# PSUM banks held by name in the second half of an attention and MLP kernel, and a last product in two banks

## The chip, the cores and the metric

The kernel runs on one core of one Trainium2 chip. The metric is the device time of one execution in microseconds (us), the median of several runs. The engines are called as in the profile: PE is TensorE (matrix products), PEld its weight loads, DVE is VectorE, ACT is ScalarE, POOL is GpSimd, SP is SyncE, which here only issues transfers.

## What is computed

Attention over a sliding window of 128 positions with a linear distance penalty, for 8 batches of 8 heads, 576 positions and a head width of 64; then, on the joined heads (512 wide), a normalised two-layer MLP with a residual:

```python
scores = scale * np.matmul(q, k.transpose(0, 1, 3, 2))
...
scores = np.where(mask, scores + bias[None], -1000000000.0)
...
attn = attn / (np.sum(attn, axis=-1, keepdims=True) + 1e-09)
return np.matmul(attn, v).astype(np.float32)
...
xn = (x - mu) / np.sqrt(var + 1e-06) * g_ln
ch = np.maximum(xn @ w_ch1, 0.0) @ w_ch2
return (x + ch).astype(np.float32)
```

## The kernel before

The 8 x 576 rows are cut into 36 blocks of 128 rows. The batches go in pairs; the ninth block of a pair holds the 64 tail rows of both batches. The blocks are gathered in twelve groups: six of two blocks, then six of four (`GROUPS`, L26). Groups are counted from 0 here, so groups 6 to 11 have four blocks.

The program is a woven one. TensorE's order, and that of ACT and DVE, is the order in which the Python code issues instructions (the manual schedule at L847 and L848). For each group, `mlp1` makes the 16 hidden tiles (L656) and a second function makes the output; both are generators that yield after each piece of matmuls. `weave_at` (L829) runs such a generator and, at listed pieces, issues the attention steps of later blocks in between: transposes of q and k, scores, the exponential on ACT, the masks on DVE, the products with the values (`values`, L415, ending in a reciprocal and a scaling on DVE), statistics, and the normalised row `xc`, which a transposing transfer turns for a later group's `mlp1`. Because all engines run in order, an instruction that waits holds up everything behind it on its engine.

In groups 6 to 11 the second layer is `fast_mlp2` (L735). It computes a 2 by 2 block product with seven products instead of eight (Winograd's scheme): sums of hidden quarters are made on DVE (`combine_hidden`, L720, eight half sums a group), sums of weight quarters once beforehand. The seven products are, in order: x, y, z, x, z, x, w. A product is 16 matmuls at L757: for each of two row blocks, 8 matmuls of 128x256 that accumulate into half a PSUM bank (a bank is 128 x 512 fp32). x collects three products, z two, y and w one each. Between them DVE adds the bank into the output tile (`add`, L767, L770), each time 128x512: x and y into one quarter, z into another, and so on. So a later product on the same bank must wait until the add before it has read the bank. The output rows go out through `send` and `store` (L777, L819), every store issued by SP, two for a block.

PSUM has eight banks. Four (`ps_sc`) are for scores and transposes of q and k. The other four are the pool `ps_mm` (L96, four buffers, tag "mm"): each hidden tile of `mlp1` (`ps_m1`, L663), each of the two value tiles of a block (`ps_pv`, L428) and each of x, y, z and w (`ps_f`, L754) takes a buffer of this pool when it is first written, and the pool decides which. In groups 6 to 10 before the change x, y, z and w came to lie in the four different banks, with value tiles in between in the banks that were free.

The order on DVE during the first products, in groups 6 to 9: scaling of the values, two hidden sums, the two masks of a block, its statistics, the add of x, a hidden sum, the row xc, the add of y, a hidden sum, the add of z.

Of the kernel before, what the change touches and what calls it, by code (L numbers as in the profile page):

```python
# [2 lines left out]

# [1 line left out]

# [6 lines left out]
FP32 = mybir.dt.float32  # L12
# [5 lines left out]
P = 128  # L18
# [6 lines left out]
HALF = P // 2  # L25
GROUPS = [2] * 6 + [4] * 6  # L26
# [32 lines left out]
def kernel(  # L59
# [10 lines left out]
    nc = tc.nc  # L70
    B, H, S, D = q.shape
    DM = H * D
# [66 lines left out]
    QF, QD = NFB // 2, DM // 2  # L139
# [181 lines left out]
    def turn_first():  # L321
# [11 lines left out]
            copy(out=k[:, b].rearrange("p h (c r) -> p r h c", r=2), in_=ps[b])  # L333
        nc.vector.tensor_copy(out=g_row, in_=ps_row)

    weights_of, unmasked, scored = {}, {}, []

    def in_halves(t):
# [80 lines left out]
    def values(p, blk, hg):  # L419

        if hg == 0:
            n = p * NSLOT + blk
            if n % 2 == 0:
                x_pairs[n // 2] = x_pool.tile([P, 2, DM], FP16, tag="x", name="x")
            xs[p, blk] = x_pairs[n // 2][:, n % 2, :]
            if n < BY_DMA:
                sums[p, blk] = small.tile([P, 2], FP32, tag="sum", name="sum")
        ps = ps_mm.tile([P, 4, D + 1], FP32, tag="mm", name="ps_pv")  # L428
        terms = weights_of[p, blk]
        for i in range(4):  # L430
            h = 4 * hg + i
            for n, (pr, t, o) in enumerate(terms):
                nc.tensor.matmul(  # L433
                    ps[:, i, :],
                    pr[:, h, t, :],
                    vext[(p * NSLOT + o) % NV][:, h, :],
                    start=(n == 0),
                    stop=(n == len(terms) - 1),
                )
        rec = small.tile([P, 4], FP32, tag="rec", name="rec")  # L440
        nc.vector.reciprocal(out=rec, in_=ps[:, :, D])  # L441
        nc.vector.scalar_tensor_tensor(  # L442
            out=xs[p, blk][:, hg * 4 * D : (hg + 1) * 4 * D].rearrange(
                "p (h d) -> p h d", h=4
            ),
            in0=ps[:, :, 0:D],
            scalar=1.0,
            in1=rec.unsqueeze(2).broadcast_to([P, 4, D]),
            op0=ALU.mult,
            op1=ALU.mult,  # L450
            **(
                dict(accum_out=sums[p, blk][:, hg : hg + 1])
                if (p, blk) in sums
                else {}
            ),
        )
# [199 lines left out]
    def mlp1(g, on_dve=()):  # L656
        xT = turned_x[g]
        w = w1 if g < FIRST_GROUPS else w1g
        cols = len(members[g]) * P
        ht = hidden[g] = hidden_pool.tile([P, NFB, 4 * P], FP16, tag="ht", name="ht")  # L660
        turn_about = chain(*zip(range(QF), range(QF, NFB)))
        for u, fb in enumerate(turn_about if g >= FAST else range(NFB)):
            ps = ps_mm.tile([P, 4 * P], FP32, tag="mm", name="ps_m1")  # L663
            for kb in range(NKB):
                nc.tensor.matmul(  # L665
                    ps[:, 0:cols],
                    w[:, kb, fb * P : (fb + 1) * P],
                    xT[:, kb, 0:cols],
                    start=(kb == 0),
                    stop=(kb == NKB - 1),  # L670
                )
            if u in on_dve:
                nc.vector.tensor_scalar(
                    out=ht[:, fb, 0:cols],
                    in0=ps[:, 0:cols],
                    scalar1=0.0,
                    scalar2=None,
                    op0=ALU.max,
                )
            else:  # L680
                nc.scalar.activation(  # L681
                    out=ht[:, fb, 0:cols], in_=ps[:, 0:cols], func=AF.Relu
                )
            yield cols
            if g >= FAST and u == 10:
                for i in range(4):
                    combine_hidden(g, 0, i)
# [47 lines left out]
    def fast_mlp2(g):  # L735

        pairs = len(members[g]) // 2
        n0 = sum(GROUPS[:g])
        outs = [out_pool.tile([P, 2, DM], FP32, tag="o", name="o") for _ in range(2)]

        def rows(i):
            if pairs == 1:
                return x_pairs[n0 // 2][:, i : i + 1, :], outs[0][:, i : i + 1, :]
            return x_pairs[n0 // 2 + i], outs[i]

        banks = {}  # L750

        def product(name, lhs, rhs, first):
            if first:
                banks[name] = ps_mm.tile([P, 2, QD], FP32, tag="mm", name="ps_f")  # L754
            for pair in range(pairs):
                for fb in range(QF):
                    nc.tensor.matmul(  # L757
                        banks[name][:, pair, :],
                        lhs[:, fb, pair * P : (pair + 1) * P],
                        rhs[:, fb, :],  # L760
                        start=(first and pair == 0 and fb == 0),
                        stop=(fb == QF - 1),
                        skip_group_check=True,
                    )
                yield DM

        def add(name, i, j, to_x):  # L767
            x, o = rows(i)
            cols = slice(j * QD, (j + 1) * QD)
            nc.vector.tensor_tensor(  # L770
                out=o[:, :, cols],
                in0=banks[name][:, 0:pairs, :],
                in1=(x if to_x else o)[:, :, cols],
                op=ALU.add,
            )

        def send(i):  # L777
            _, o = rows(i)
            for at in range(pairs):
                store(*members[g][i * pairs + at], o[:, at, :])  # L780

        a = [[hidden_quarter(g, i, j) for j in range(2)] for i in range(2)]
        s = [hidden_sum(g, i) for i in range(4)]
        combine_hidden(g, 1, 0)
        combine_hidden(g, 1, 1)
        yield from product("x", a[0][0], quarter(0, 0), True)
        add("x", 0, 0, True)
        combine_hidden(g, 1, 2)
        yield from product("y", a[0][1], quarter(1, 0), True)
        add("y", 0, 0, False)  # L790
        combine_hidden(g, 1, 3)
        yield from product("z", s[0], t1, True)
        add("z", 1, 1, True)
        yield from product("x", s[1], t2, False)
        add("x", 0, 1, True)
        yield from product("z", s[3], quarter(1, 1), False)
        add("z", 0, 1, False)
        send(0)
        yield from product("x", s[2], t3, False)
        add("x", 1, 0, True)  # L800
        add("x", 1, 1, False)
        yield from product("w", a[1][1], t4, True)
        add("w", 1, 0, False)
        send(1)

    def finish(p, blk, ps):
        n = p * NSLOT + blk
# [8 lines left out]
        )  # L816
        store(p, blk, o)

    def store(p, blk, o):  # L819
        for b, t0, w, p0 in spans(p, blk):  # L820
            dst, src = out[b, t0 : t0 + w, :], o[p0 : p0 + w, :]
            if blk == T:
                nc.sync.dma_start(out=dst, in_=src)
            else:
                dst = dst.rearrange("(c r) d -> r c d", r=2)
                for r in range(2):
                    nc.sync.dma_start(out=dst[r], in_=src[r * HALF : (r + 1) * HALF])

    def weave_at(units, *places, also=()):  # L829
        for u, _ in enumerate(units):  # L830
            advance_to(done + places.count(u))
            if u in also:
                next(combined, None)
# [13 lines left out]
    with tc.manual_schedule(engines={engine.PE}):  # L847
        with tc.manual_schedule(engines={engine.Activation, engine.DVE}):  # L848
            advance_to(first)
            weave_at(mlp1(0, (0, 1)), 2, 7, 8, 9, 13)  # L850
            weave_at(mlp1(1), 2, 8, 12)
            weave_at(mlp2(0, ((0, 8), (8, 12), (12, NFB))), 0, 1, 3, 4, 4, 5)
            weave_at(mlp2(1), 0, 1, 2, 3, 4, 6, 6)
            weave_at(mlp1(2), 0, 3, 3, 6, 8, 11)
            weave_at(mlp2(2), 0, 2, 4, 6, 7)


            weave_at(mlp1(3, (9, 10, 11)), 8, 8, 12, 13)
            weave_at(mlp2(3), 0, 1, 1, 2, 4, 4, 5, 6)
            weave_at(mlp1(4), 0, 4, 8, 10, 10, 14)  # L860
            weave_at(mlp2(4), 0, 2, 2, 3, 5, 7, also=(1, 4, 6))
            weave_at(mlp1(5), 0, 1, 4, 8, 10, 12, also=(3, 6, 9))
            weave_at(mlp2(5), 0, 1, 2, 4, 6, 7)
            for g in range(6, len(GROUPS)):
                weave_at(
                    mlp1(g), 0, 2, 5, 7, 8, 10, 13, 15, also=(1, 4) if g == 6 else ()
                )
                weave_at(fast_mlp2(g), 1, 3, 6, 7, 7, 9, 12, 13)
# [31 lines left out]
```

## Time and profile before

| what | us |
|---|---|
| median of 3 runs | 334.84 (334.58 to 335.43) |
| the profiled execution's own time | 334.56 |
| its span, first to last instruction | 332.8 |
| `mlp1` matmuls with 512 columns (L665, 640) | 116.9 busy, 1.1 idle before |
| `fast_mlp2` matmuls (L757, 384 + 192 + 96) | 45.8 + 22.5 + 11.5 busy, 8.7 idle before |
| the adds out of PSUM in `fast_mlp2` (L770, 24 + 24) | 16.4 + 16.4 busy |
| stores (72), issue to landing | 2.4 |

Busy time is the time in which an engine had an instruction running; idle before a group of instructions is the time its engine stood still just ahead of them, with the engine that ended the wait. The mean granted clock of TensorE over the span is 0.99 of full speed. A matmul of 128x512 starts 0.216 us after the one before it, one of 128x256 0.109 us.

### The profile page before, as it was taken

Reading aid. Unit: us, or ns where it says so; the run is one execution under the profiler, and the core shown is the slowest. Engines: PE = TensorE matmul, PEld = TensorE weight load, DVE = VectorE, ACT = ScalarE, POOL = GpSimd, SP = SyncE. Lnnn points to the kernel's source line nnn. Section 1 sums busy time; section 2 is a strip of 40 time slices with the busy share of each in tenths; the row PEclk is TensorE's granted clock in tenths of the full one; section 3 lists DMA queues with packets and bytes.
Section 4 is the critical chain, followed back from the end, with each engine's and each line's share of the span. In section 5 each row is a group of like instructions: output and inputs, shape, how many; then the busy total and the mean of one; then the engine's idle time right before and its main releaser. Section 6 shows DMA issues by size and latency. Waiting matters only on the chain.

```text
span 332.8 us, 10421 instructions
## 1 busy us (share of the span) xinstructions
PE 309.3 (93%) x4478; PEld 208.2 (63%) x4478; DVE 234.4 (70%) x555; ACT 184.6 (55%) x320; POOL 114.8 (35%) x188
## 2 busy tenths in 40 slices
PE   8889999998999999999799979999899979999992
PEld 3478556757567575558655866567656854685582
DVE  2879777786777887669775986589758975761462
ACT  6688666676656583684278533763287218405600
POOL 8933677666425652813252541300000000000000
PEclk9999999999999999999999997999999999999998
DMA  9999999999599696996396966351430033015005
GB/s 112 167 207 191 189 152 195 173 140 146 47 145 96 76 157 58 160 66 65 42 164 86 97 65 98 85 43 18 81 81 18 18 80 82 18 23 121 0 2 126
DMA packets 101728, 32.34 MB, mean 97 GB/s; under 512 B 92849, under 2 KB 97073, under 8 KB 101682
## 3 DMA queue, kind: packets, MB, share of 16 engines
q0 software_dynamic: 79872, 18.36, 64.9%
q1 hardware_dynamic: 21810, 13.32, 19.4%
q8 instruction: 35, 0.57, 0.8%
q14 instruction: 11, 0.09, 0.1%
HBM read 36.90 MB, written 9.44 MB: 139 GB/s over the span
## 4 chain that ended last, share of the span: by engine, by line
PE 71%; DVE 10%; ACT 7%; POOL 4%; DMA 4%; issue 2%; DVEq 0%; POOLq 0%; ACTq 0%
PE ps_m L665 31%; PE ps_f L757 21%; PE ps_m L698 9%; ACT probs L389 4%; DMA w<-in_moe_w_ch_dram 4%; PE ps_sc L381 4%; PE ps_pv L433 4%; PE ps_sc L277 2%; DVE probs L400 2%; DVE st L530 2%; POOL vx L223 1%; DVE o L770 1%; POOL q L213 1%; DVE k L297 1%; POOL rstd L488 1%
## 5 line engine op out<-in xcount | busy, mean ns | idle before, releaser
L665 PE MATMUL ps_m<-xT,w1g 128*128 128x512 f16 (+1 forms) x640 | 116.9, 337 | 1.1 <-ACT ht L681 0.8
L681 ACT ACTIVATE ht<-ps_m 128x512 f16<-128x512 f32 (+1 forms) x187 | 89.2, 497 | 39.6 <-PE ps_m L665 36.7
L665 PEld LDWEIGHTS <-w1g 128*128 128x128 f16 x640 | 60.1, 98 | 48.8 <-issue 1.8
L389 ACT ACTIVATE probs<-ps_sc 128x1024 f16<-128x1024 f32 x56 | 54.3, 1026 | 39.7 <-PE ps_sc L381 39.7
L757 PE MATMUL ps_f<-w,ht 128*128 128x256 f16 x384 | 45.8, 279 | 8.7 <-DVE o L770 8.7
L757 PEld LDWEIGHTS <-ht 128*128 128x128 f16 x384 | 37.9, 100 | 14.9 <-issue 9.4
L485 POOL TENSOR_TENSOR rstd<-moments,powers 128x1 f32<-128x1 f32 x28 | 5.4, 192 | 118.6 <-DVE moments L531 118.6
L698 PE MATMUL ps_m<-w,ht 128*128 128x512 f16 x192 | 46.0, 380 | 0.0
L223 POOL DMA_DIRECT2D vx<-in_v_dram x40 | 34.7, 880 | 26.7 <-PE ps_pv L433 12.5
L400 DVE TENSOR_TENSOR probs<-probs,m 128x1024 f16<-128x1024 f16 x56 | 37.4, 688 | 9.1 <-ACT probs L389 8.7
L213 POOL DMA_DIRECT2D q<-in_q_dram x40 | 27.3, 688 | 20.2 <-PE ps_sc L277 12.0
L442 DVE SCALAR_TENSOR_TENSOR x<-ps_pv,rec 128x256 f16<-128x256 f32 x72 | 30.6, 425 | 2.5
L213 POOL DMA_DIRECT2D k<-in_k_dram x40 | 26.9, 686 | 5.9 <-DMA w<-in_moe_w_ch_dram 3.6
L698 PEld LDWEIGHTS <-ht 128*128 128x128 f16 x192 | 17.1, 98 | 17.4
L472 DVE TENSOR_SCALAR xc<-x,moments,rstd 128x512 f16<-128x512 f16 x28 | 11.5, 412 | 19.9 <-POOL rstd L488 19.9
L530 DVE BATCH_NORM_STATS2 st<-x 128x6 f32<-128x512 f16 x36 | 24.6, 685 | 0.0
L296 ACT COPY q<-ps_sc 128x512 f16<-128x512 f16 x15 | 8.8, 586 | 28.0 <-PE ps_sc L277 27.8
L381 PE MATMUL ps_sc<-q,k 64*64 64x128 f16 (+1 forms) x1088 | 20.4, 208 | 3.8 <-ACT probs L389 1.1
L441 DVE RECIPROCAL rec<-ps_pv 128x4 f32<-128x4 f32 x72 | 12.7, 176 | 15.9 <-PE ps_pv L433 15.5
L757 PE MATMUL ps_f<-w,hs 128*128 128x256 f16 x192 | 22.5, 273 | 0.0
L770 DVE TENSOR_TENSOR o<-ps_f,x 128x512 f32<-128x512 f32 x24 | 16.4, 684 | 7.6 <-PE ps_f L757 7.5
L433 PEld LDWEIGHTS <-probs 128*128 128x128 f16 x448 | 18.7, 97 | 4.7 <-DVE probs L400 0.3
(79 smaller groups left out, 345.5 us busy)
## 6 DMA issues: line engine op xcount, KB each, us to landing
out_dram<-o SPq DMA_DIRECT2D x72, 128.0 KB, 2.4
q<-in_q_dram POOLq DMA_DIRECT2D x32, 128.0 KB, 5.2
k<-in_k_dram POOLq DMA_DIRECT2D x32, 128.0 KB, 5.6
vx<-in_v_dram POOLq DMA_DIRECT2D x32, 128.0 KB, 6.5
w<-in_moe_w_ch_dram POOLq DMA_DIRECT2D x8, 512.0 KB, 10.7
q<-in_q_dram POOLq DMA_DIRECT2D x8, 64.0 KB, 4.7
k<-in_k_dram POOLq DMA_DIRECT2D x8, 64.0 KB, 4.5
vx<-in_v_dram POOLq DMA_DIRECT2D x8, 64.0 KB, 5.9
```

What stands on the lines that cost most here:

```text
L213: nc.gpsimd.dma_start(out=t[b * n // 2 : (b + 1) * n // 2], in_=src[2 * p + b, :, i * P : i * P + n, :].rearrange("h (c r) d -> c h r d", ...
L223: nc.gpsimd.dma_start(out=vx[p0 : p0 + n, :, 0:D], in_=v[b, :, t0 : t0 + n, :].rearrange("h p d -> p h d"),)
L381: nc.tensor.matmul(in_halves(ps[cols, j, n, t, :])[:, r, queries], kt[rows, hp, cols], in_halves(qt[rows, b, hp])[:, r, queries], start=Tr ...
L389: nc.scalar.activation(out=dst.rearrange("p (n j) q -> p j n q", j=2), in_=ps.rearrange("p j n t q -> p j n (t q)"), func=AF.Exp, scale=in ...
L400: nc.vector.tensor_tensor(out=dst, in0=dst, in1=mask, op=ALU.mult)
L433: nc.tensor.matmul(ps[:, i, :], pr[:, h, t, :], vext[(p * NSLOT + o) % NV][:, h, :], start=(n == 0), stop=(n == len(terms) - 1),)
L442: nc.vector.scalar_tensor_tensor(out=xs[p, blk][:, hg * 4 * D : (hg + 1) * 4 * D].rearrange("p (h d) -> p h d", h=4), in0=ps[:, :, 0:D], s ...
L530: nc.vector.bn_stats(out=st, in_=xs[order[n]])
L665: nc.tensor.matmul(ps[:, 0:cols], w[:, kb, fb * P : (fb + 1) * P], xT[:, kb, 0:cols], start=(kb == 0), stop=(kb == NKB - 1),)
L681: nc.scalar.activation(out=ht[:, fb, 0:cols], in_=ps[:, 0:cols], func=AF.Relu)
L698: nc.tensor.matmul(sums[at], ht[:, fb, at * P : (at + 1) * P], w2[:, fb, :], start=(fb == 0), stop=(fb == NFB - 1),)
L757: nc.tensor.matmul(banks[name][:, pair, :], lhs[:, fb, pair * P : (pair + 1) * P], rhs[:, fb, :], start=(first and pair == 0 and fb == 0), ...
```

## The change

From group 6 on, the four buffers of `ps_mm` are allocated once, as four tiles that are never given back (`ring`), and a function `psum` hands them out: the first of the list, which then goes to its end. Hidden tiles and value tiles take the next of the list. At the start of `fast_mlp2` the first two become the bank of x and the bank of y, and **z uses the bank of y**; the other two stay in the list for value tiles, and w is written into the first of those. Behind the sixth product the list is put together again: second other bank, y, x, first other bank.

In the last group w's two halves go to two different banks, its add is made in two halves of 128x256, and the last two blocks are stored by columns: the right halves after the sixth product, the left half of each block after its add. These stores are issued by SP and ACT in turn. All other stores stay with SP.

```diff
+    ring = []
+    def psum(name, banks=None):
+        if not ring:
+            return ps_mm.tile([P, DM], FP32, tag="mm", name=name)
+        t = (banks or ring)[0]
+        if banks is None:
+            ring.append(ring.pop(0))
+        return t
...
-        ps = ps_mm.tile([P, 4, D + 1], FP32, tag="mm", name="ps_pv")
+        ps = psum("ps_pv")[:, 0 : 4 * (D + 1)].rearrange("p (h d) -> p h d", h=4)
...
-            ps = ps_mm.tile([P, 4 * P], FP32, tag="mm", name="ps_m1")
+            ps = psum("ps_m1")
...
-        banks = {}
+        x_bank, y_bank, *others = ring
+        use = dict(x=[x_bank] * 2, y=[y_bank] * 2, z=[y_bank] * 2, w=others[:1] * 2)
+        if g == len(GROUPS) - 1:
+            use["w"] = others
+        ring[:] = others
+        banks = {
+            name: [b.rearrange("p (j d) -> p j d", j=2) for b in bs]
+            for name, bs in use.items()
+        }
...
-            if first:
-                banks[name] = ps_mm.tile([P, 2, QD], FP32, tag="mm", name="ps_f")
...
-                        banks[name][:, pair, :],
+                        banks[name][pair][:, pair, :],
...
-                        start=(first and pair == 0 and fb == 0),
+                        start=(
+                            first
+                            and fb == 0
+                            and (pair == 0 or use[name][0] is not use[name][1])
+                        ),
...
-        def add(name, i, j, to_x):
+        def add(name, i, j, to_x, at=slice(0, pairs)):
...
-        def send(i):
+        def send(i, ats=range(pairs), cols=slice(0, DM), queues=(nc.sync,)):
...
-        yield from product("w", a[1][1], t4, True)
-        add("w", 1, 0, False)
-        send(1)
+        if use["w"][0] is use["w"][1]:
+            ring[:] = [others[1], y_bank, x_bank, others[0]]
+            yield from product("w", a[1][1], t4, True)
+            add("w", 1, 0, False)
+            send(1)
+        else:
+            low, high = slice(0, QD), slice(QD, DM)
+            send(1, cols=high, queues=(nc.sync, nc.scalar))
+            for at, _ in enumerate(product("w", a[1][1], t4, True)):
+                add("w", 1, 0, False, slice(at, at + 1))
+                send(1, [at], low, (nc.sync, nc.scalar))
+                yield DM
...
-    def store(p, blk, o):
+    def store(p, blk, o, cols=slice(0, DM), queues=(nc.sync,)):
+        queues = cycle(queues)
...
+            ring += [ps_mm.tile([P, DM], FP32, tag="mm", name="ps_r") for _ in range(4)]
             for g in range(6, len(GROUPS)):
```

More of the change, by code (lines that the diff above doesn't have):

```diff
@@ L1 @@
 from contextlib import ExitStack
-from itertools import chain
+from itertools import chain, cycle
 import numpy as np
@@ L770, in add @@
             nc.vector.tensor_tensor(
-                out=o[:, :, cols],
-                in0=banks[name][:, 0:pairs, :],
-                in1=(x if to_x else o)[:, :, cols],
+                out=o[:, at, cols],
+                in0=banks[name][at.start][:, at, :],
+                in1=(x if to_x else o)[:, at, cols],
                 op=ALU.add,
             )
-        def send(i):
+        def send(i, ats=range(pairs), cols=slice(0, DM), queues=(nc.sync,)):
             _, o = rows(i)
-            for at in range(pairs):
-                store(*members[g][i * pairs + at], o[:, at, :])
+            for at in ats:
+                store(*members[g][i * pairs + at], o[:, at, :], cols, queues)
         a = [[hidden_quarter(g, i, j) for j in range(2)] for i in range(2)]
@@ L817, in finish @@
         store(p, blk, o)
-    def store(p, blk, o):
+    def store(p, blk, o, cols=slice(0, DM), queues=(nc.sync,)):
+        queues = cycle(queues)
         for b, t0, w, p0 in spans(p, blk):
-            dst, src = out[b, t0 : t0 + w, :], o[p0 : p0 + w, :]
+            dst, src = out[b, t0 : t0 + w, cols], o[p0 : p0 + w, cols]
             if blk == T:
-                nc.sync.dma_start(out=dst, in_=src)
+                next(queues).dma_start(out=dst, in_=src)
             else:
@@ L826, in store @@
                 for r in range(2):
-                    nc.sync.dma_start(out=dst[r], in_=src[r * HALF : (r + 1) * HALF])
+                    next(queues).dma_start(
+                        out=dst[r], in_=src[r * HALF : (r + 1) * HALF]
+                    )
     def weave_at(units, *places, also=()):
```

## The prediction

> **What bounds the kernel now.** I read the page's busy shares first, then TensorE's waits from 150 us to the end (groups of four blocks start at 135.3 us), the timeline of one group, the windows with the granted clock, and the timeline of the tail. The busy shares:
>
> ```profile
> PE 309.3 (93%) x4478; PEld 208.2 (63%) x4478; DVE 234.4 (70%) x555; ACT 184.6 (55%) x320; POOL 114.8 (35%) x188
> ```
>
> TensorE's waits after 150 us (who for whom; us in all, times, longest):
>
> ```profile
> PE ps_f L757 <- DVE o L770: 8.7, 4, 2.2
> PE ps_sc L381 <- DVE rec L441: 0.4, 1, 0.4
> ```
>
> That is 9.1 us in 183. TensorE is the bound, it runs its queue in order, and there is almost no slack into which a new wait could fall: what is added on TensorE here arrives at the end. The 8.7 us are four waits of 2.14, 2.24, 2.11 and 2.20 us, one in each of groups 6 to 9, all at the sixth product. The timeline of group 7 (start, duration, engine, line; a bracket gives the idle time before it):
>
> ```profile
> 186.06 3.67 PE L757 MATMUL ps_f<-w,ht 128*128 128x256 f16 x32
> 189.56 2.78 PE L757 MATMUL ps_f<-w,hs 128*128 128x256 f16 x24
> 189.91 0.69 DVE L770 TENSOR_TENSOR o<-ps_f,x 128x512 f32<-128x512 f32 x1
> 190.52 0.68 DVE L733 TENSOR_TENSOR w<-ht,hs 128x1024 f16<-128x1024 f16 x1
> 191.12 0.41 DVE L472 TENSOR_SCALAR xc<-x,moments,rstd 128x512 f16<-128x512 f16 x1
> 191.44 0.68 DVE L770 TENSOR_TENSOR o<-ps_f,o 128x512 f32<-128x512 f32 x1
> ...
> 198.20 0.66 DVE L770 TENSOR_TENSOR o<-ps_f,x 128x512 f32<-128x512 f32 x1
> 198.92 5.32 PE L757 MATMUL ps_f<-w,ht 128*128 128x256 f16 x32 [2.24 <-DVE o L770]
> ```
>
> The 32 matmuls at 186.06 are products x and y; z starts at 189.56 at once, since it has a bank of its own. VectorE is behind: it adds x at 189.91 and y only at 191.44 to 192.12. The sixth product (x again) waits for the add that reads x's bank, which ends at 198.86; TensorE goes on at 198.92, some 0.05 us after.
>
> **z in y's bank.** From group 6 on, z gets the bank of y. Its first matmul (start set) then cannot be issued before the add of y has read that bank; in the changed program's instruction order it carries that wait, and VectorE's order is unchanged: the add of y still stands behind the masks, the statistics, the add of x, a hidden sum and xc. So z starts 0.05 us after the add of y ends. From the timelines (z's start now; end of the add of y):
> - group 6: 155.48; 157.32 + 0.68 = 158.00: 2.57 us
> - group 7: 189.56; 192.12: 2.61
> - group 8: 225.20; 227.29 + 0.68 = 227.97: 2.82
> - group 9: 259.26; 261.24 + 0.68 = 261.92: 2.71
> - group 10: 291.98; 293.22 + 0.69 = 293.91: 1.98
> - group 11: 318.02; 318.22 + 0.69 = 318.91: 0.94
>
> Together 13.63 us. Behind z in TensorE's queue stand the fourth product, the values and scores of the next block, and the rest. Nothing takes the delay back: the sixth product's wait hangs on a chain that TensorE itself starts after the fourth product (scores, two ACT exponentials, masks, statistics, add of x). In group 6 VectorE idles 0.21 us for the values, then 0.42 and 0.22 us for ACT, so it follows TensorE there and is not working off a backlog; the chain moves with z and the 8.7 us stay.
>
> **The w bank in the next group.** w takes the first of the two other banks, and the ring afterwards is values' bank, y, x, w. Behind w come two values tiles, so the next group's first hidden tile goes to x and its second to w's bank. VectorE adds w only after the values. The second tile would start four matmuls of 0.216 us (0.864) after the first: at 170.25, 205.98, 239.93 and 273.96 for groups 7 to 10; the adds end at 170.56, 206.30, 240.24 and 274.38. With 0.05 us each: 0.36 + 0.37 + 0.36 + 0.47 = 1.56 us. Before, that bank came fourth in groups 7 to 10, 1.7 us later, which hid the add; that cover is gone. Group 11 has no values behind w, its fourth tile takes w's bank, and it costs nothing there.
>
> **The held tiles.** With one tile per bank for the rest of the program, a reciprocal also waits for the ACT that read its bank before: always long done, but one more semaphore instruction on VectorE, two per values step. The rows for such instructions run 21 to 50 ns. The two before z in each of groups 6 to 10 lie on VectorE's way to the add of y: between 0 and 10 x 0.05 = 0.5 us; I take 0.25. The ACT ones are hidden in the 0.27 us ACT idles between two hidden tiles.
>
> **The tail.** Timeline of the last group's end:
>
> ```profile
> 324.18 4.60 SPq L827 DMA_DIRECT2D out_dram<-o  x6
> ...
> 325.82 0.68 DVE L770 TENSOR_TENSOR o<-ps_f,o 128x512 f32<-128x512 f32 x1
> 326.96 0.69 DVE L770 TENSOR_TENSOR o<-ps_f,o 128x512 f32<-128x512 f32 x1 [0.46 <-PE ps_f L757]
> 328.83 1.24 SPq L823 DMA_DIRECT2D out_dram<-o  x2
> ```
>
> The last add ends at 327.65; SP then issues four stores one after the other (0.6 us and a small step each), the last at 329.48, which lands 2.4 us later. After the change the last product's halves lie in two banks, the first half is added beside the second's matmuls, and the add that remains is 128x256 (estimate 0.40 us, near the 0.42 us of the 128x256 row that reads PSUM on L442): done at 327.36. Eight stores of half the bytes go out, four on each queue. SP is busy with the stores of the first two blocks until 326.58, then issues at about 326.6, 327.25, 327.9 and 328.55: 0.93 us earlier than 329.48. No trace row has ACT issuing a transfer. If it costs what SP's do, ACT ends with SP; if it costs POOL's 0.88 us (L223), its fourth starts near 326.55 + 3 x 0.9 = 329.25 and only 0.23 is saved; if also the smaller transfer lands 0.3 us sooner than 2.4 (estimate), 1.25 is saved. SP's rows are the nearer ones, the same stores out of the same tiles, where POOL's are loads with a change of type: I take 0.95.
>
> **The clock.** Windows of 3.41 us, laid so that the stretch at half clock fills one (busy us by engine, then the granted clock):
>
> ```profile
> 162.25:165.66 3.41, 1.56 (x15) 1.40 (x15) 2.77 (x6) 0.00 (x0) 0.74 (x2) 1.00 0.46 27
> 196.38:199.79 3.41, 1.17 (x12) 0.89 (x11) 2.78 (x7) 0.36 (x1) 0.97 (x3) 1.00 0.93 68
> 199.79:203.20 3.41, 3.41 (x19) 2.43 (x17) 1.75 (x3) 0.00 (x0) 0.00 (x0) 0.50 0.49 102
> 230.51:233.92 3.41, 1.91 (x21) 1.57 (x17) 2.86 (x8) 1.84 (x2) 0.00 (x0) 1.00 0.00 0
> ```
>
> In group 7 the 2.24 us gap fell whole into one window (TensorE busy 1.17 of 3.41), and the next window ran at 0.50: 32 matmuls took 5.32 us where groups 8 and 9 show 3.65. That is 1.67 us. The other three gaps straddled a window's edge (busy 1.56 and more) and cost none. So the limit lies between 1.85 and 2.24 us idle in a window; I take 2.05. A gap of g us at a random phase has that much in one window with chance (3.41 + g - 4.10)/3.41: 0.58 for the four new gaps (mean 2.68), 0.43 for the four old ones (2.17), none for 1.98 and 0.94. That is 2.3 + 1.7 = 4.1 slow windows where before had one: 3.1 more; with the limit at 2.24, 2.4 more, at 1.86, 4.0. Before drew one where this formula gives 1.7, and its times lie within 0.9 us of each other, less than a slow window's cost; so I take the low side, 2.5 more: 2.5 x 1.67 = 4.2 us, with 0 and 7 x 1.67 = 11.7 as ends.
>
> The Trainium skill ("TensorE: Matmul & The Clock Gate", section "Why this matters for your kernels") asks only that TensorE not idle longer than about 3 us between bursts; by it none of these gaps would cost clock and the sum would be 349.0. The trace differs: 2.24 us were enough. The same page's section "A second HAM failure mode: psum-queue depth-cycling" speaks against this change: cycling through PSUM banks with small TensorE gaps made the clock swing there. The half-speed window after the gap agrees with it.
>
> **Sum**, against the profiled execution's 334.56 us (its span 332.8 and 1.8 around it; 0.28 under the median of 334.84): 334.56 + 13.63 + 1.56 + 0.25 - 0.95 = 349.05; + 4.2 for the clock = 353.3 us.
>
> **Rivals.**
> - The same waits, clock no worse: 349.0. For it: three of the four old gaps cost nothing. Against: the new gaps are 0.4 us longer, and there are four more.
> - A slow window after nearly every gap: 349.05 + 11.7 = 360.7. Against: three of four now go free.
> - The new wait replaces the old one: if the add of x in the fourth product's wake hung on VectorE's own backlog, TensorE would find it done: 349.05 - 8.7 = 340.4. For it: VectorE works without a break from 185.4 to 194.2 in group 7. Against: the idle gaps for values and ACT just before that add.
> - Not slower: the add of y is through before z wants its bank. It decides only if VectorE gets there 2.5 us sooner than now; then 13.63 and 0.25 fall away, 334.56 + 1.56 - 0.95 = 335.2, and without w's wait 333.6. Against: VectorE's order is the same and its row back to back. This is also the case in which the new bank names bind nothing.
>
> **How the numbers follow.** Forecast 353.3: 0.58, its own range 350.5 to 357.5. Clock no worse 0.20, slow windows everywhere 0.10, wait replaced 0.09, not slower 0.03. The range 347.8 to 357.5 takes in the first two and, with the tail's 0.23 to 1.25 and the semaphores' 0 to 0.5, leaves the rest out, about 0.2. About 0.3% (1 us) is what a measurement here tells from no change. Faster by more than that (333.6): 0.01; within it (335.2): 0.02; slower: 0.97.
>
> **What would show it.** Right: TensorE waits for the add on z's first matmul, six times, 13 to 14 us, the longest in groups 6 to 9; the four old waits still near 2.2 us; four of about 0.4 us at a group's second hidden tile; three or four windows at 0.50; last stores issued by SP and ACT, the last about 1 us nearer to the last matmul. Wrong: the waits at the sixth product shrink as those at z grow; or no wait at z; or the time beyond 357.5 with more slow windows than four.

## The result and the profile after

The changed kernel took 353.52 us (median of four runs: 348.92, 351.00, 356.04, 357.52). Beside it the kernel before took 334.71 (median of four). The ratio is 1.047, with an interval of 1.037 to 1.057; it leaves out the two slower of the four runs, which lie over 1.5% above the fastest, so it comes out below the ratio of the two medians. The profiled execution is the longest of the four, 357.52 us with a span of 355.7.

The page of the changed kernel, its busy shares, the row of the granted clock and two groups of matmuls (busy, mean ns of one, idle time before and who ended it):

```profile
PE 319.1 (90%) x4478; PEld 211.9 (60%) x4478; DVE 235.8 (66%) x556; ACT 184.9 (52%) x320; POOL 114.8 (32%) x188
...
PEclk9999999999999999988899899998999889999999
...
L775 PE MATMUL ps_r<-w,ht 128*128 128x256 f16 x384 | 49.0, 290 | 8.7 <-DVE o L792 8.7
...
L775 PE MATMUL ps_r<-w,hs 128*128 128x256 f16 x192 | 27.1, 307 | 12.9 <-DVE o L792 12.9
```

The matmuls are as many as before (4478). The busy time of PE is 9.8 us longer with the same work, most of it a slower clock; all dips of the clock's row lie in the groups of four. The 8.7 us of waiting ahead of the products that read `ht` (all at the sixth) are unchanged, and 12.9 us have come up ahead of the products that read `hs`, where before had none. z is the first of these.

TensorE's waits of the changed kernel from 150 us on (who for whom; us in all, times, longest):

```profile
PE ps_r L775 <- DVE o L792: 21.7, 10, 2.7
PE ps_r L677 <- DVE o L792: 0.9, 4, 0.3
PE ps_sc L393 <- DVE rec L453: 0.4, 1, 0.4
```

The ten waits at the products are the four old ones and six new ones. The four on L677 are the second hidden tile of groups 7 to 10. Group 7 in the timeline of the changed kernel (start, duration, engine, line; the bracket is the idle time before it):

```profile
192.39 3.67 PE L775 MATMUL ps_r<-w,ht 128*128 128x256 f16 x32
...
196.32 0.69 DVE L792 TENSOR_TENSOR o<-ps_r,x 128x512 f32<-128x512 f32 x1
196.93 0.68 DVE L745 TENSOR_TENSOR w<-ht,hs 128x1024 f16<-128x1024 f16 x1
197.52 0.41 DVE L484 TENSOR_SCALAR xc<-x,moments,rstd 128x512 f16<-128x512 f16 x1
197.84 0.69 DVE L792 TENSOR_TENSOR o<-ps_r,o 128x512 f32<-128x512 f32 x1
198.45 0.68 DVE L745 TENSOR_TENSOR ht<-ht 128x1024 f16<-128x1024 f16 x1
198.58 4.45 PE L775 MATMUL ps_r<-w,hs 128*128 128x256 f16 x24 [2.52 <-DVE o L792]
...
209.60 3.65 PE L775 MATMUL ps_r<-w,ht 128*128 128x256 f16 x32 [2.24 <-DVE o L792]
```

DVE does the same things in the same order as before: the add of x, a hidden sum, xc, and only then the add of y (197.84 to 198.53). z starts 0.05 us after that add, where before it followed the y product at once. The sixth product, 11 us later, still waits its 2.24 us.

Windows of 3.41 us of the changed kernel, laid against the stretches at half clock (busy us of PE, PEld, DVE, ACT and POOL, then the granted clock, DMA share and GB/s):

```profile
164.85:168.26 3.41, 1.39 (x13) 1.09 (x12) 2.73 (x6) 1.35 (x2) 0.62 (x3) 1.00 0.67 46
168.26:171.67 3.41, 3.29 (x16) 2.30 (x16) 1.08 (x3) 0.00 (x0) 0.40 (x1) 0.50 0.21 41
195.57:198.98 3.41, 0.89 (x9) 0.65 (x7) 3.38 (x7) 0.00 (x0) 0.75 (x2) 1.00 0.34 20
198.98:202.39 3.41, 3.41 (x18) 2.46 (x17) 0.69 (x2) 0.00 (x0) 0.00 (x0) 0.50 0.22 43
...
311.60:315.03 3.43, 1.55 (x15) 1.24 (x14) 3.37 (x8) 0.00 (x0) 0.74 (x2) 1.00 0.00 0
315.03:318.44 3.41, 3.41 (x34) 3.05 (x32) 0.98 (x2) 0.00 (x0) 0.00 (x0) 1.00 0.20 38
```

Up to the last matmul, six windows of this execution ran at half clock, against one in the profiled execution of before. Ahead of each of the six stood a window in which TensorE was busy for 0.89 to 1.39 us (1.20, 1.39, 0.89, 1.29, 1.18, 1.21); the windows with 1.55 us or more had none behind them.

The tail of the changed kernel (the queues' rows show when a store is issued and how long that takes):

```profile
349.55 1.56 DVE L792 TENSOR_TENSOR o<-ps_r,o 128x512 f32<-128x512 f32 x3
350.26 0.57 ACTq L859 DMA_DIRECT2D out_dram<-o  x1
...
352.22 0.56 ACTq L855 DMA_DIRECT2D out_dram<-o  x1
352.50 0.56 SPq L855 DMA_DIRECT2D out_dram<-o  x1
```

An issue by ACT takes 0.55 to 0.61 us, like one by SP. From the end of the last matmul to the end of the span it is 5.09 us (350.65 to 355.74) where before took 5.87 (326.92 to 332.79).

### The profile page after: what moved, and what is told of

Read it like the earlier page. It is cut to its first block, busy times and chain, and to the rows that moved or that the text cites. A ratio compares the mean times of both kernels' runs of the same rounds, so it can differ in the third digit from the quotient of the medians.

```text
span 355.7 us, 10469 instructions
## 1 busy us (share of the span) xinstructions
PE 319.1 (90%) x4478; PEld 211.9 (60%) x4478; DVE 235.8 (66%) x556; ACT 184.9 (52%) x320; POOL 114.8 (32%) x188
## 4 chain that ended last, share of the span: by engine, by line
PE 56%; DVE 23%; ACT 6%; DMA 5%; POOL 5%; issue 4%; DVEq 0%; POOLq 0%; ACTq 0%
PE ps_r L677 17%; PE ps_r L775 17%; PE ps_m L710 8%; PE ps_m L677 7%; ACT probs L401 4%; DVE probs L412 4%; DMA w<-in_moe_w_ch_dram 4%; DVE hs L745 3%; DVE st L542 3%; DVE o L792 3%; PE ps_sc L393 2%; DVE x L454 2%; PE ps_sc L277 2%; PE ps_r L445 2%; DMA q<-in_q_dram 1%
## 5 line engine op out<-in xcount | busy, mean ns | idle before, releaser
L677 PEld LDWEIGHTS <-w1g 128*128 128x128 f16 x640 | 60.1, 98 | 50.3 <-issue 3.8
L677 PE MATMUL ps_r<-xT,w1g 128*128 128x512 f16 x384 | 86.1, 380 | 0.9 <-DVE o L792 0.9
L693 ACT ACTIVATE ht<-ps_r 128x512 f16<-128x512 f32 x96 | 56.4, 599 | 33.6 <-PE ps_r L677 33.6
L775 PE MATMUL ps_r<-w,ht 128*128 128x256 f16 x384 | 49.0, 290 | 8.7 <-DVE o L792 8.7
L775 PEld LDWEIGHTS <-ht 128*128 128x128 f16 x384 | 39.4, 104 | 16.8 <-issue 9.4
L775 PE MATMUL ps_r<-w,hs 128*128 128x256 f16 x192 | 27.1, 307 | 12.9 <-DVE o L792 12.9
L693 ACT ACTIVATE ht<-ps_m 128x256 f16<-128x256 f32 x91 | 33.1, 388 | 9.2 <-PE ps_m L677 6.5
L677 PE MATMUL ps_m<-xT,w1g 128*128 128x256 f16 x256 | 31.4, 273 | 1.1 <-ACT ht L693 0.8
L792 DVE TENSOR_TENSOR o<-ps_r,x 128x512 f32<-128x512 f32 x24 | 16.5, 686 | 23.1 <-PE ps_r L775 23.1
L775 PEld LDWEIGHTS <-hs 128*128 128x128 f16 x192 | 20.7, 109 | 18.4 <-issue 14.0
L710 PEld LDWEIGHTS <-ht 128*128 128x128 f16 x192 | 17.1, 98 | 17.4
```

Source lines behind the costliest of these rows:

```text
L677: nc.tensor.matmul(ps[:, 0:cols], w[:, kb, fb * P : (fb + 1) * P], xT[:, kb, 0:cols], start=(kb == 0), stop=(kb == NKB - 1),)
L693: nc.scalar.activation(out=ht[:, fb, 0:cols], in_=ps[:, 0:cols], func=AF.Relu)
L710: nc.tensor.matmul(sums[at], ht[:, fb, at * P : (at + 1) * P], w2[:, fb, :], start=(fb == 0), stop=(fb == NFB - 1),)
L775: nc.tensor.matmul(banks[name][pair][:, pair, :], lhs[:, fb, pair * P : (pair + 1) * P], rhs[:, fb, :], start=(first and fb == 0 and (pair ...
L792: nc.vector.tensor_tensor(out=o[:, at, cols], in0=banks[name][at.start][:, at, :], in1=(x if to_x else o)[:, at, cols], op=ALU.add,)
```

## The experiments

The theory: z in y's bank makes TensorE wait for the add of y, and w's bank second in the next group makes it wait for the add of w; the gaps so made cost clock as well; the tail gains a little. The rivals: something else in the change (tiles that are held, the other order of banks) makes the loss, or the clock is slow for a reason of its own. The kernel before, on the same chip, took 333.90 us (median of 19 runs, 332.09 to 337.37) beside the first four kernels, and 334.64 (7 runs, 333.67 to 337.51) beside the last four.

### The change with a bank of its own for z

```diff
-        x_bank, y_bank, *others = ring
-        use = dict(x=[x_bank] * 2, y=[y_bank] * 2, z=[y_bank] * 2, w=others[:1] * 2)
+        x_bank, y_bank, z_bank, *others = ring
+        use = dict(x=[x_bank] * 2, y=[y_bank] * 2, z=[z_bank] * 2, w=others[:1] * 2)
+        others.append(y_bank)
...
-            ring[:] = [others[1], y_bank, x_bank, others[0]]
+            ring[:] = [y_bank, z_bank, x_bank, others[0]]
```

> The changed kernel with one thing undone: z gets a bank of its own again, as before; banks still held by name, w's bank still second in the next group, tail as changed. Theory (the time was lost because z's first matmul waits for the add of y): no wait at z, the four old waits at the sixth product stay near 2.2 us, the four at the second hidden tile stay near 0.2 us (0.9 us in all), one or two half-clock windows: 334.56 + 0.9 - 1.0 = 334.5 us, between 333 and 336.5 by the number of half-clock windows. Rival (the held tiles and their fixed turn are what costs, with more semaphores on every engine): stays above 345.

Measured: 336.70 us (median of ten, 333.67 to 339.32), ratio 1.007 (1.002 to 1.011). TensorE's waits after 150 us in this kernel:

```profile
PE ps_r L776 <- DVE o L793: 8.6, 4, 2.2
PE ps_r L677 <- DVE o L793: 0.9, 4, 0.3
```

No wait at z; the four at the sixth product and the four at the second hidden tile stay. The held tiles and the list are the same as in the changed kernel, so they are not what costs 14 us. The median is above the expected 334.5 because some runs lost clock: the two runs with a mean clock of 0.999 took 333.67 and 334.05, the three with 0.986 and 0.985 took 338.29 to 339.32.

The profiled execution (333.67 us) had no window at half clock, so positions can be compared with before, where the one window's 1.67 us are taken off from group 8 on. The sixth product of groups 6, 7, 8 and 9 starts at 164.10, 199.32, 233.62 and 268.11 us, before at 164.09, 198.92, 232.85 and 266.99; the last block of matmuls starts at 323.17 against 321.59. So the four waits for w's bank cost 0.39, 0.37, 0.35 and 0.46 us, 1.57 in all, though the trace lists them as 0.9. Nothing but these waits is left between the two kernels on the way there. In this kernel the semaphores of the held tiles cost nothing that can be seen, but nothing in it waits for the add of y, on whose way they lie.

### The kernel before with z in y's bank, and nothing else

```diff
-                banks[name] = ps_mm.tile([P, 2, QD], FP32, tag="mm", name="ps_f")
+                banks[name] = (
+                    banks["y"]
+                    if name == "z"
+                    else ps_mm.tile([P, 2, QD], FP32, tag="mm", name="ps_f")
+                )
```

> The kernel before with one thing of the change: z is written into y's bank; nothing is held by name, tail as before. Theory: six waits at z of together 12.9 us as in the changed kernel's trace (2.41, 2.52, 2.73, 2.62, 1.88, 0.78), the four old ones stay, 1 to 5 half-clock windows more: 334.56 + 12.9 = 347.5 us without further half-clock windows, 349 to 356 with them. Rival (held tiles cost, the shared bank is hidden): within 1 us of the kernel before.

Measured: 351.99 us (median of four, 349.89 to 354.94), ratio 1.058 (1.051 to 1.064). Its clock row, its waits after 150 us, and z of group 7:

```profile
PEclk9999999999999999998899889999999989999997
```

```profile
PE ps_f L761 <- DVE o L774: 21.4, 10, 2.7
...
198.19 4.42 PE L761 MATMUL ps_f<-w,hs 128*128 128x256 f16 x24 [2.45 <-DVE o L774]
```

One shared bank in the kernel before, whose pool is otherwise as it was, brings the whole loss, dips of the clock included (five windows in the profiled execution). Its last block of matmuls starts at 343.62 us, before at 323.26. Of these 20.36 us, 0.30 are a later start of the groups (135.59 against 135.29) and 6.68 four more windows of 1.67 us, which leaves 13.4 for the six waits. Counted from starts (from y's first matmul to z's, less the 1.75 us which that takes before) the six waits are 2.57, 2.62, 2.83, 2.71, 1.98 and 0.94 us, 13.65 together. The two kernels together settle the main cause: with the shared bank the loss is there without the rest of the change, and without it the rest of the change loses little.

### The tail alone

The kernel before, with the last group's w in two banks, its add in halves, and the last two blocks stored by columns from SP and ACT in turn, as in the change.

> The kernel before with the tail of the change alone: the last product in two banks, its add in two halves, the last stores by columns and issued by SP and ACT in turn. Theory: from the end of the last matmul to the end of the span about 1.0 us less than before, every other wait unchanged: 333.6 us, or 332 where no half-clock window falls. Rival (eight smaller stores cost as much as four large ones): 334.6, the last landing no earlier.

Measured: 333.99 us (median of ten, 332.86 to 337.33) against 333.90, ratio 1.005 (1.001 to 1.008). In the trace the end after the last matmul is 5.07 us, 0.80 less than before. The time doesn't show it: four of the ten runs lie at 336.41 to 337.33, with a mean clock of 0.982 to 0.986, and the other six between 332.86 and 334.10 (the 334.10 with 0.985 as well). The profiled one of the four (336.71) began its groups 1.23 us later than before and had one more window at half clock in them: from the first group of four to the last block of matmuls it is 189.68 us against 187.97. So the time of this edit is covered by things that it doesn't touch, and for the tail the trace alone speaks.

### The change with TensorE kept busy while it waits

Matmuls of 128x512 that nobody reads, 91 in all, are put in front of z (11 in groups 6 to 9, then 8 and 3) and in front of the sixth product (9 in groups 6 to 9). Each set lasts a little less than the wait behind it.

```diff
+        def fill(n):
+            for _ in range(n):
+                nc.tensor.matmul(others[0], ones[:, 0:P], ones, start=True, stop=True)
...
+        fill({10: 8, 11: 3}.get(g, 11))
...
+        fill(9 if g < 10 else 0)
```

> The changed kernel with throw-away matmuls (128x512, into a bank that is free then) put on TensorE in its gaps: 11 before z in groups 6 to 9, 8 and 3 in groups 10 and 11, and 9 before the sixth product in groups 6 to 9, each set a little shorter than the gap it lies in. Theory (a gap of over about 2 us in one clock window halves the clock in the next, and that is what spreads the changed kernel's runs from 349 to 357.5): no half-clock window after the start-up, all runs within 1 us of each other, at 334.56 - 1.67 (the one window of before) + 12.9 + 0.9 - 1.0 = 345.7 us, up to 346.5 if the fillers overrun a gap a little. Rival (the clock does not follow TensorE's idle time): half-clock windows as often as in the changed kernel, 349 us or more and as wide a spread; if the fillers did not fit into the gaps, up to 91 x 0.216 = 19.7 us more.

Measured: 348.36 us (median of four, 347.46 to 350.45), ratio 1.046 (1.041 to 1.052). The clock row of this kernel, and its waits after 150 us:

```profile
PEclk9999999999999999999999999999999999999998
```

```profile
PE ps_r L775 <- DVE o L792: 1.9, 8, 0.4
PE ps_r L677 <- DVE o L792: 0.9, 4, 0.3
```

The products still start when the adds let them, but the dips are gone: in the groups the clock falls because TensorE stands idle, not by itself. The four runs now lie within 3.0 us, those of the changed kernel within 8.6. What is left is the waits themselves. From the first group of four to the last block of matmuls it is 201.75 us here (136.06 to 337.81); before, without its one slow window, it is 187.97 - 1.67 = 186.30. So z and w's bank cost 15.45 us with no window at half clock in either figure. With that, 334.56 - 1.67 + 15.45 - 0.8 gives 347.5, and the fastest run is 347.46. The profiled run (349.07) began its groups 0.77 us later and ended 5.74 us behind its last matmul, where one of SP's issues took 1.29 us. The expected 345.7 to 346.5 was too low because it used the waits as the trace lists them.

### The change with w's bank last in the next group

```diff
             ring[:] = [others[1], y_bank, x_bank, others[0]]
             yield from product("w", a[1][1], t4, True)
             add("w", 1, 0, False)
             send(1)
+            ring[:] = [x_bank, others[1], y_bank, others[0]]
```

> The changed kernel with the ring put together so that w's bank comes fourth in the next group's hidden tiles, as before, and not second. Theory: the four waits at the second hidden tile vanish and from the start of a group's hidden tiles to its ninth product step nothing else moves; 1.56 us less than the changed kernel at the same number of half-clock windows: 347.2 + 1.67 for each such window in the groups - 1.56. Rival (the wait is hidden by ACT, which is behind there): no difference in the stretch from one group's hidden tiles to the next.

Measured: one run of 351.52 us. The waits on L677 for the adds are gone from the trace, the ten at the products stay at 21.7 us:

```profile
PE ps_r L775 <- DVE o L792: 21.7, 10, 2.7
PE ps_sc L393 <- DVE rec L453: 0.4, 1, 0.4
```

From the first group of four to the last block of matmuls it is 205.21 us against 211.54; three windows at half clock less account for 5.01, which leaves 1.32 us for w's bank. The time of one run says nothing here.

### The kernel before with the add of x issued earlier

The wait at the sixth product was there before the change. In Python, the add of x after the fourth product is issued behind the next block's reciprocals, masks and statistics; here it is issued as soon as the product's last matmul is.

```diff
-        yield from product("x", s[1], t2, False)
-        add("x", 0, 1, True)
+        fourth = product("x", s[1], t2, False)
+        yield next(fourth)
+        next(fourth)
+        add("x", 0, 1, True)
+        yield DM
```

> The kernel before, with one instruction moved on VectorE: the add of x after the fourth product stands ahead of the next block's reciprocals, masks and statistics, instead of behind them. Theory (these waits are VectorE's queue order, not its load, and each also risks a half-clock window): the four waits at the sixth product vanish, 8.7 us and some 0.1 us each that the trace's modelled matmul ends hide, and no half-clock window falls in the groups: 334.56 - 1.67 - 9.1 = 323.8 us, within 1.5 us from run to run. Rival (VectorE is the bound there, and the wait comes back at the next add, the masks or the values): 331 to 334.

Measured: 326.61 us (median of four, 325.88 to 327.67), ratio 0.976 (0.973 to 0.980). Group 7 of this kernel in the timeline, and its waits after 150 us:

```profile
191.95 1.05 PE L757 MATMUL ps_f<-w,hs 128*128 128x256 f16 x8
...
193.22 0.67 DVE L770 TENSOR_TENSOR o<-ps_f,x 128x512 f32<-128x512 f32 x1
...
193.79 1.92 PE L757 MATMUL ps_f<-w,w 128*128 128x256 f16 x16
193.81 0.17 DVE L441 RECIPROCAL rec<-ps_pv 128x4 f32<-128x4 f32 x1
...
195.54 3.66 PE L757 MATMUL ps_f<-w,ht 128*128 128x256 f16 x32
```

```profile
PE ps_sc L381 <- DVE rec L441: 1.3, 2, 1.0
PE ps_m L665 <- DVE o L770: 1.0, 3, 0.4
```

The add of x (193.22) now stands ahead of the reciprocals (193.81), and the sixth product (195.54, no bracket) starts without a wait. Some of the gain comes back: one wait of 0.96 us at the scores, which start 0.06 us after DVE's copy of k (167.17 to 167.88; the row names the reciprocal behind it), and 0.33, 0.23 and 0.42 us at hidden tiles whose banks DVE reads later than before, 1.94 us together as listed. From the first group of four to the last block it is 179.37 us, before 187.97 - 1.67 = 186.30: 6.93 us saved where 9.1 were expected. Counted from starts the four old waits were 9.4 us, so some 2.5 came back. No window in the groups ran at half clock any more.

### Both: the early add of x and the tail

> The kernel before with the add of x moved ahead as in the other run, and the tail of the change: 0.8 us less than that run, 323.0 us. If the tail's gain is hidden elsewhere: equal to that run.

Measured: 324.50 us (median of four, 324.10 to 325.56), ratio 0.970 (0.967 to 0.974). This is the fastest version found, 10 us under the kernel before. TensorE is busy for 307.4 us, 95% of the span.

The end after the last matmul is 5.07 us here, 5.86 without the tail. The medians differ by 2.1 us, more than these 0.8. In the profiled runs (324.10 against 326.27) the rest is the start-up: the groups began at 134.36 us against 135.61, 1.25 us earlier, and from there to the last block of matmuls the two are within 0.2 us of each other. The tail's edit changes nothing ahead of the last group.

### The change with the adds of x and y issued earlier

The early add of x as above, and in the same way the add of y right behind its product, ahead of a hidden sum and of xc.

```diff
-        combine_hidden(g, 1, 2)
-        yield from product("y", a[0][1], quarter(1, 0), True)
+        second = product("y", a[0][1], quarter(1, 0), True)
+        yield next(second)
+        next(second)
...
+        combine_hidden(g, 1, 2)
+        yield DM
```

> The changed kernel (z in y's bank) with VectorE's order mended at both places: the add of x after the fourth product ahead of the next block's work, and the add of y ahead of one hidden sum and of xc (0.60 + 0.32 us). Theory: z's waits lose 0.92 us in groups 6 to 10 and nothing in group 11, 13.6 - 4.6 = 9.0 us stay; the waits at the sixth product vanish (9.1); the gaps that are left, 1.0 to 1.9 us, are mostly too short for half-clock windows: 334.56 - 1.67 - 9.1 + 9.0 + 1.56 - 0.8 = 333.5 us, up to 337 if the longest gap (group 8) still halves the clock. Rival (the bank alone sets z's wait, whatever VectorE's order): z's waits stay at 13.6 us and the time near 338.

Measured: 338.38 us (median of four, 337.87 to 338.79), ratio 1.011 (1.007 to 1.015). Its waits after 150 us:

```profile
PE ps_r L775 <- DVE o L792: 9.3, 6, 2.0
PE ps_r L677 <- DVE o L792: 3.0, 6, 0.7
PE ps_sc L393 <- DVE rec L453: 1.3, 2, 1.0
```

The waits at z are 1.68, 1.79, 2.00, 1.89, 1.15 and 0.78 us, against 2.41, 2.52, 2.73, 2.62, 1.88 and 0.78 in the changed kernel: 0.73 less in each of the first five, expected 0.92. The two adds of group 6 show the rest:

```profile
156.44 0.69 DVE L792 TENSOR_TENSOR o<-ps_r,x 128x512 f32<-128x512 f32 x1
157.23 0.69 DVE L792 TENSOR_TENSOR o<-ps_r,o 128x512 f32<-128x512 f32 x1
```

The add of y reads the rows of `o` that the add of x writes. Right behind it, it starts 0.79 us after it, 0.10 after its end. Where the next instruction doesn't read what the one before wrote, it starts ahead of that end: in the changed kernel 0.61 us lie between the starts of the add of x and the hidden sum (196.32, 196.93), and of two adds into different quarters (348.94, 349.55). The difference of 0.18 us is about what is missing. The sixth product waits no more, and no window in the groups ran at half clock. So the length of z's wait is a matter of where the add of y stands in DVE's order, and that it waits at all is a matter of the bank. With the shared bank the kernel stays 14 us behind the kernel with the early add of x and the tail (324.50); the adds that remain late now hold up hidden tiles (0.67 us each in three groups, besides 0.33, 0.26 and 0.41). It is also above the expected 333.5 to 337: counted from starts z's waits are 10.3 us where 9.0 were put down, and those at the hidden tiles have grown.

## Why the prediction was right, point by point

- **z in y's bank: right, in kind and in size.** Six waits, at z's first matmul, each ended by the add of y. The prediction had 13.63 us. Counted from starts they are 13.65 us with z in y's bank alone, and 13.93 in the changed kernel. The changed kernel's brackets list them as 2.41, 2.52, 2.73, 2.62, 1.88 and 0.78 us, 12.94 together, which is 1.0 less: the trace models a matmul's end, and draws a matmul of 128x256 as 0.27 us though the next starts 0.109 us after it, so an idle time after matmuls is listed too short. Reading the wait from starts, as the prediction did, gave the right size.
- **w's bank: right.** Four waits at the second hidden tile, predicted 1.56 us, 1.57 by the positions in the kernel with a bank for z, 1.32 by the kernel with w's bank last.
- **The old waits stay: right.** 2.14, 2.24, 2.14 and 2.20 us at the sixth product, as before. The rival in which the new wait replaces the old (340.4) falls, for the reason given: the add of x there hangs on work that starts behind the fourth product. The early add bears this out: with the add of x taken out of that queue, the wait is gone.
- **The held tiles: right, in kind and in size.** 0.25 us were put down for semaphore instructions on VectorE's way to the add of y. The changed kernel has 20 more of these on VectorE than before, all at the reciprocals (L453), of 21 ns; with z in y's bank alone there are none. z's waits in groups 7 to 10 are 2.52, 2.73, 2.62 and 1.88 us against 2.45, 2.67, 2.55 and 1.81 there, 0.27 more together, while group 6 has 2.41 in both. In group 7 the first reciprocal starts 0.07 us later against TensorE's matmuls than it does there.
- **The tail: nearly right.** 0.95 us predicted, 0.78 in the changed kernel (5.87 less 5.09) and 0.80 alone. ACT's issues cost what SP's do, as chosen. The mis-sized part is the time of the last issue: it was to come 0.93 us earlier, and counted from the last matmul's end it comes 0.71 earlier (352.50 - 350.65 = 1.85 us behind it, before 329.48 - 326.92 = 2.56).
- **The clock: the mechanism right, the size within its spread.** The prediction had 2.5 windows more than before. It named, as a sign that it is wrong, a time beyond 357.5 us with more than four slow windows, and the profiled execution, 357.52 us with six, is such a run. By mean clock (0.971, 0.972, 0.987, 0.992; one window of 3.41 us at half clock takes 0.005 off, and the half clock behind the last matmul up to as much) the four runs had about six, six, two or three, and one or two. The median falls between the two pairs, so that it came out at 353.5 against 353.3 is partly luck. The rival "clock no worse" (349.0) describes the fastest run, 348.92 us at a mean clock of 0.992, where the profiled execution of before has 0.990; it falls for the other three runs and for the median. In the working, the formula with the limit at 2.24 gives 2.2 windows more and not 2.4, and with 1.86 it gives 4.5 and not 4.0, since group 10's gap of 1.98 us then counts too.
- **The limit for a slow window** was put at 2.05 us idle, between 1.85 and 2.24. The changed kernel narrows it: 1.39 us busy of 3.41, so 2.02 idle, was enough; 1.55 busy, so 1.86 idle, was not. In the kernel with the tail alone 1.44 busy, so 1.97 idle, was not either (267.96 to 271.37 us). This holds for the groups of four only: in that kernel's profile and in that of the change with the early adds, one window in the first 20 us ran at half clock behind one that was busy for 2.18 and 2.08 us, with other matmuls, mostly scores and transposes. What sets the limit there stays open.

The terms close. The last block of matmuls starts at 346.99 us, before at 323.26: 23.73 us later. Of these 13.93 are z with the held tiles, 1.57 w's bank and 0.16 a later start of the groups (135.45 against 135.29). The 8.07 that are left for five more windows are 1.61 each, a little under the 1.67 that was taken; in three of the six slow windows TensorE was busy for 3.22, 3.29 and 3.38 of the 3.41 us only. The filled kernel closes with no window: 15.45 us measured, 13.63 + 0.25 + 1.56 = 15.44 predicted.

The Trainium skill ("TensorE: Matmul & The Clock Gate", section "Why this matters for your kernels") asks that TensorE not idle longer than about 3 us between bursts. By it the changed kernel would have kept its clock; the trace differs, gaps of 2.1 to 2.7 us cost it six windows. The same page's section "What's actually happening" has a window of 3413 ns that runs freely and doesn't start with the kernel; with that the stretches of 3.41 us agree, and so does a number of slow windows that changes from run to run. The skill ("Perfetto Trace Analysis", section "Matmuls") also says that independent groups of matmuls should rotate through different PSUM banks, so that the read of one overlaps the next; the kernel with a bank for z agrees, with 336.7 us against 353.5.

## What to carry to other kernels

A PSUM bank that is used again turns the place of its reader in another engine's queue into a wait of TensorE: before sharing one, look up when that read ends in the timeline, and subtract the start that the next matmul would have had. If a wait is there, moving the read up in its engine's order can be worth more than a bank (the early add of x and the tail: 324.5 us). Then add the clock: here a gap in which about 2 us of idle time fell into one window cost 1.6 to 1.7 us more, and made the time vary from run to run.

## What was not expected of the hardware

- The spread between runs of the changed kernel is mostly the draw of slow windows. With the gaps filled by matmuls that nobody reads, four runs lay within 3.0 us instead of 8.6; these 91 matmuls are listed as 21.3 us of work, and the time is shorter.
- A wait after matmuls is listed 0.1 to 0.2 us too short. For the four waits at w's bank (listed 0.19 to 0.29, by positions 0.35 to 0.46) that is half of them.
- The start-up also varies: the first group of four began at 135.29, 135.45, 135.61, 135.77 and 136.06 us in the profiles of before, after, the early add, w's bank last and the filled kernel, and at 134.36 and 136.52 in those of both (early add and tail) and of the tail alone, though none of these edits touches what runs before it. In the latest of them, the tail's, one window at half clock lies in the start-up. What else sets the start stays open.
